# Induced attention and an ELU feed-forward on one core: which engine takes off the 1 of 1+elu, and where it is made up for

## The chip, the cores and the metric

One core of one Trainium2 chip. The engines run side by side and meet through semaphores: TensorE (PE, matmuls into PSUM, the memory of the matmul sums), VectorE (DVE), ScalarE (ACT), GpSimd (POOL, which works on SBUF, the main on-chip memory) and SyncE (SP, which here issues the DMA transfers). The metric is device microseconds of one execution; lower is better.

## The reference

```python
B, N, m, C = 4, 12480, 32, 128                     # x: (B, N, C), inducing: (m, C)
def mab(q, kv):
    s = scale * (q @ kv.transpose(0, 2, 1))
    s = s - s.max(-1, keepdims=True)
    a = np.exp(s)
    a /= a.sum(-1, keepdims=True) + 1e-09
    return a @ kv
h = mab(I, x)                                      # 32 rows look at all of x
x = mab(x, h).reshape(B * N, C)                    # every token looks at those 32 rows
h = x @ w_in                                       # (49920, 128) @ (128, 2048)
g = np.where(h > 0.0, h, np.exp(np.minimum(h, 0.0)) - 1.0)
return (g @ w_out).astype(np.float32)              # (49920, 2048) @ (2048, 128)
```

x and inducing are float32; the two weights are float64 and are put into float32 on the chip. Nearly all of the work is the last three lines.

## The kernel before

**Tiles.** The tokens of a batch are cut into 25 blocks, 15 of 512 and 10 of 480 (GROUPING), so there are 60 and 40 blocks in the four batches. The 2048 hidden columns are 16 chunks of 128, taken in pairs. A *unit* is one block and one pair (8 units a block, 800 in all), and nearly all instructions work on a unit's tile of 128 x 1024 (or 960).

**A unit.** `ffn_in` (L618) makes ph = h + 1 with two matmuls in PSUM (the 1 comes from rows of ones in `hw` and in the stacks; w_in is folded into the 32 attended rows, so the contraction has 128 rows). ACT then makes e = exp(ph - 1) (L626). `ffn_mid` (L632, DVE) makes min(max(ph, 1), e), which is 1 + elu(h). The rest depends on the pair's letter in PLAN:

- N: POOL subtracts 1 in place (L653), and e goes as it is, float32, into two full matmuls with `wo_n`. The profile shows a float32 matmul as two instructions.
- P and D are *split*: ACT writes gh, elu rounded to F32R, a shorter float32 that PE takes in one instruction (`ffn_split`, L641, bias -1), then somebody writes the remainder gl, and the product is summed from gh x wo_h, gh x wo_l and gl x wo_h: six matmuls a unit. For D, DVE makes gl = (g - 1) - gh (L648); here `ffn_mid` has written g over ph, so L648 reads PSUM and SBUF, and the PSUM tile stays taken until then. For P, POOL first subtracts 1 in place (L653), then makes gl = e - gh (L658).

PLAN is PDNPDPND: three P, three D, two N. Chunks of P and D have their places in `wo_h` and `wo_l` (CHUNKS_S), those of N in `wo_n`. All 16 chunks of a block are summed in one PSUM bank, `po` (L680), one of two that take turns. After the eighth pair DVE transposes `po` into `o` in SBUF (L688), and SP writes it out with four DMAs (L692).

**Order.** PE, DVE and ACT run in the order in which the program is written; POOL and SP are put in order by the framework, and tiles are handed out from pools: three PSUM tiles for ph, five for e, four for gh, four for gl, two for o. One step of the unit loop issues `ffn_in(n)` with its exponential, `ffn_mid(n - 1)`, `ffn_split(n - 1)`, `ffn_low(n - 2)`, what is due of the attention steps, and `ffn_out(n - 5)`. So ACT's queue is exponential n, split n - 1; DVE's is L632 of n - 1, L648 of n - 2.

**Attention.** The two attentions of the next batch and the next groups of blocks are side steps with written due times in units of blocks (`attend`, `first_half`). The second attention comes per group of two to four blocks and uses POOL three times: subtracting the maximum (L550), dividing (L570), and the remainder of the rounded weights (L591); stacks of weights are then copied by DMA (L596).

**Start.** The first 105 us or so make the float32 weights out of the float64 bits (class `Weight`, `split_w_out`) and the first attention of batch 0, in the order of the text FIRST; DVE and POOL have instructions there with two operands in SBUF (L198, L208, L212, L239).

Of the kernel before, what the change touches and what calls it, by code (L numbers as in the profile page):

```python
# [9 lines left out]
F32 = mybir.dt.float32  # L10
F32R = mybir.dt.float32r
I32 = mybir.dt.int32
U32 = mybir.dt.uint32
AF = mybir.ActivationFunctionType
# [4 lines left out]
Q = 32  # L19
# [5 lines left out]

PLAN = "PDNPDPND"

# [13 lines left out]
def kernel(  # L45
# [28 lines left out]
    NFC = F // P  # L74
    NCP = NFC // 2
    assert len(PLAN) == NCP
    CHUNKS_S = [f for f in range(NFC) if PLAN[f // 2] != "N"]
    CHUNKS_N = [f for f in range(NFC) if PLAN[f // 2] == "N"]
    WHERE_S = {f: i for i, f in enumerate(CHUNKS_S)}
    WHERE_N = {f: i for i, f in enumerate(CHUNKS_N)}  # L80
# [34 lines left out]
    def bank(name, take=False):  # L115
        if not steady and not take:
            return ps_h.tile([P, 2, 512], F32, tag="ph", name=name)[:, 0]
        t = ps_o.tile([P, 512], F32, tag=f"po{turn[0] % 2}", name=name)
        if take:
            turn[0] += 1  # L120
        return t
# [29 lines left out]
    wo_n = const.tile([P, len(CHUNKS_N), C], F32, name="wo_n")  # L151
    wo_h = const.tile([P, NSPLIT, C], F32R, name="wo_h")
    wo_l = const.tile([P, NSPLIT, C], F32R, name="wo_l")
    WS = 512
    rebias = const.tile([P, 1], F32, name="rebias")
    nc.gpsimd.memset(rebias, -896.0)
# [451 lines left out]
    def plan(n):  # L608
        b, k, cp = units[n]
        return PLAN[cp]  # L610
# [17 lines left out]

    def ffn_mid(n):
        v = live[n]  # L630
        v["g"] = v["ph"] if plan(n) == "D" else v["e"]
        nc.vector.scalar_tensor_tensor(  # L632
            out=v["g"], in0=v["ph"], scalar=1.0, in1=v["e"], op0=ALU.max, op1=ALU.min
        )

    def ffn_split(n):
        v, how = live[n], plan(n)
        shape = list(v["e"].shape)
        if how != "N":
            v["gh"] = ghp.tile(shape, F32R, tag="gh", name=f"gh_{n}")  # L640
            nc.scalar.activation(v["gh"], v["g"], AF.Copy, bias=-1.0)  # L641

    def ffn_low(n):
        v, how = live[n], plan(n)
        shape = list(v["e"].shape)
        if how == "D":
            v["gl"] = glp.tile(shape, F32R, tag="gl", name=f"gl_{n}")
            nc.vector.scalar_tensor_tensor(  # L648
                out=v["gl"], in0=v["g"], scalar=-1.0, in1=v["gh"].bitcast(F32),
                op0=ALU.add, op1=ALU.subtract,  # L650
            )
        else:
            nc.gpsimd.tensor_scalar(  # L653
                out=v["e"], in0=v["e"], scalar1=-1.0, scalar2=1.0, op0=ALU.add, op1=ALU.mult
            )
        if how == "P":
            v["gl"] = glp.tile(shape, F32R, tag="gl", name=f"gl_{n}")
            nc.gpsimd.tensor_sub(v["gl"], v["e"], v["gh"].bitcast(F32))  # L658

    def ffn_out(n):  # L660
        b, k, cp = units[n]
# [7 lines left out]
        for i in range(2):  # L669
# [3 lines left out]
            else:  # L673
# [2 lines left out]
                parts.append((1, wo_l[:, w, :], v["gh"][:, i]))  # L676
                parts.append((2, wo_h[:, w, :], v["gl"][:, i]))
        parts.sort(key=lambda v: v[0])
        for i, (_, w, g) in enumerate(parts):
            nc.tensor.matmul(  # L680
                po[:, :T], w, g,
                start=(cp == 0 and i == 0),
                stop=(cp == NCP - 1 and i == len(parts) - 1),
            )
        if cp == NCP - 1:
            yield 1
            o = op.tile([P, U, Q], F32, tag="o", name=f"o_{b}_{k}")
            nc.vector.transpose(o.rearrange("p u d -> p (u d)"), po[:, :T])  # L688
            at = b * N + BLOCKS[k][0]
            dst = out[at : at + T, :]  # L690
            for dq in range(4):
                nc.sync.dma_start(  # L692
                    dst[:, dq * Q : (dq + 1) * Q].rearrange("(u t) d -> t u d", t=Q),
                    o[dq * Q : (dq + 1) * Q, :, :],
                )
# [194 lines left out]
```

## Time and profile before

| | us |
|---|---|
| median of 3 runs | 1710.24 |
| lowest, highest | 1710.19, 1712.89 |
| span of the profiled execution | 1710.8 |

| engine | busy us | share of the span | instructions |
|---|---|---|---|
| PE (matmuls) | 1656.3 | 97% | 7448 |
| PEld (weight loads, beside the matmuls) | 1176.5 | 69% | 7448 |
| DVE | 1522.5 | 89% | 1575 |
| ACT | 1390.6 | 81% | 1620 |
| POOL | 1342.3 | 78% | 948 |

Times in rows are microseconds unless marked ns. A row of the groups reads: line, engine, operation, tile written <- tiles read, shapes, count | busy time, mean ns of one | idle time of the engine before them, and what ended it. A row of the timeline reads: start, duration, engine, line, operation, tiles, shapes, count. A row of waits reads: who <- whom: microseconds in all, times, longest. The stretch view gives each engine's busy time in a stretch with its count of instructions. A matmul's end is modelled, so what one costs is read from start to start.

### The profile page before, as it was taken

What the parts mean: (1) busy time and instruction counts of PE and PEld (TensorE: products, weight loads), DVE (VectorE), ACT (ScalarE), POOL (GpSimd) and SP (SyncE); (2) the same over time, 40 slices, a digit from 0 to 9 for tenths busy, and PEclk for the clock granted to TensorE, in tenths of its full rate; (3) what the DMA queues carried; (4) which work ended last, traced back from release to release, by engine and by line L of the source; (5) the groups of instructions that cost most, each with busy time, mean ns of one, the idle gap of its engine ahead of it and who ended that gap; (6) DMA issues with size and microseconds to landing.
All of it is one profiled execution on the core that took longest, in us unless ns stands there. A gap on an engine that the chain in (4) does not pass through costs nothing.

```text
span 1710.8 us, 22335 instructions
## 1 busy us (share of the span) xinstructions
PE 1656.3 (97%) x7448; PEld 1176.5 (69%) x7448; DVE 1522.5 (89%) x1575; ACT 1390.6 (81%) x1620; POOL 1342.3 (78%) x948
## 2 busy tenths in 40 slices
PE   6589999999999999999999999999999999999998
PEld 4356776677776776767776676677777677777776
DVE  5799899898899998988989999889888989998996
ACT  4378888888787888888888888888878888888886
POOL 4488787787797877877888787787778888888886
PEclk9699999999999999999999999999999999999999
DMA  7144223322324233232223332321222111111111
GB/s 249 35 91 80 56 43 78 63 48 70 70 46 83 37 75 70 45 62 58 71 64 54 65 62 53 75 55 21 74 49 40 35 20 36 28 37 19 36 25 19
DMA packets 384754, 98.10 MB, mean 57 GB/s; under 512 B 364864, under 2 KB 370784, under 8 KB 384384
## 3 DMA queue, kind: packets, MB, share of 16 engines
q1 hardware_dynamic: 384640, 96.68, 27.9%
q8 instruction: 59, 0.97, 0.2%
q14 instruction: 55, 0.45, 0.1%
HBM read 48.94 MB, written 25.56 MB: 44 GB/s over the span
## 4 chain that ended last, share of the span: by engine, by line
PE 87%; DVE 7%; ACT 3%; issue 2%; DMA 1%; POOL 0%; SPq 0%; DVEq 0%; ACTq 0%
PE po L680 62%; PE ph L618 20%; ACT e L626 2%; DVE e L632 1%; PE ps_s L312 1%; PE ps_t L531 1%; PE ps_hh L403 1%; DVE ph L632 1%; ACT gh L641 1%; DMA xm<-in_x_dram 1%; DVE o L688 1%; DVE w_part L198 1%; DVE gl L648 0%; DMA w_raw<-in_moe_w_in_dram 0%; PE ps_hw L467 0%
## 5 line engine op out<-in xcount | busy, mean ns | idle before, releaser
L626 ACT ACTIVATE e<-ph 128x1024 f32<-128x1024 f32 (+1 forms) x800 | 803.4, 1005 | 228.8 <-PE ph L618 223.7
L653 POOL TENSOR_SCALAR e<-e 128x1024 f32<-128x1024 f32 (+1 forms) x500 | 510.8, 1029 | 280.6 <-ACT gh L641 270.4
L658 POOL TENSOR_TENSOR gl<-e,gh 128x1024 fp32r<-128x1024 f32 (+1 forms) x300 | 703.8, 2346 | 16.8
L632 DVE SCALAR_TENSOR_TENSOR e<-ph,e 128x1024 f32<-128x1024 f32 (+1 forms) x500 | 594.5, 1189 | 88.0 <-ACT e L626 84.9
L618 PE MATMUL ph<-stk,hw 128*128 128x512 f32 (+1 forms) x1600 | 566.8, 436 | 15.8 <-DVE e L632 9.6
L680 PE MATMUL po<-gh,wo_h 128*128 128x512 f32 (+1 forms) x1200 | 469.2, 391 | 7.5 <-ACT wo_h L238 3.5
L680 PE MATMUL po<-gh,wo_l 128*128 128x512 f32 (+1 forms) x1200 | 469.3, 391 | 6.6 <-POOL wo_l L239 6.6
L618 PEld LDWEIGHTS ph<-stk,hw 128*128 128x128 f32 x1600 | 295.4, 189 | 188.9 <-issue 84.9
L632 DVE SCALAR_TENSOR_TENSOR ph<-ph,e 128x1024 f32<-128x1024 f32 (+1 forms) x300 | 359.3, 1198 | 63.1 <-ACT e L626 62.3
L680 PE MATMUL po<-gl,wo_h 128*128 128x512 f32 (+1 forms) x1200 | 371.1, 390 | 0.7 <-POOL gl L658 0.7
L680 PE MATMUL po<-e,wo_n 128*128 128x512 f32 (+1 forms) x800 | 367.8, 582 | 0.1
L648 DVE SCALAR_TENSOR_TENSOR gl<-ph,gh 128x1024 fp32r<-128x1024 f32 (+1 forms) x300 | 356.3, 1188 | 1.0 <-ACT gh L641 1.0
L641 ACT ACTIVATE gh<-e 128x1024 fp32r<-128x1024 f32 (+1 forms) x300 | 311.3, 1038 | 13.9 <-DVE e L632 13.5
L641 ACT ACTIVATE gh<-ph 128x1024 fp32r<-128x1024 f32 (+1 forms) x300 | 300.6, 1002 | 19.1 <-DVE ph L632 18.2
L680 PEld LDWEIGHTS po<-gh,wo_h 128*128 128x128 f32 x1200 | 225.9, 188 | 56.6 <-issue 7.4
L680 PEld LDWEIGHTS po<-gh,wo_l 128*128 128x128 f32 x1200 | 225.9, 188 | 56.5 <-POOL wo_l L239 8.2
L680 PEld LDWEIGHTS po<-gl,wo_h 128*128 128x128 f32 x1200 | 225.6, 188 | 49.1 <-POOL gl L658 1.7
L680 PEld LDWEIGHTS po<-e,wo_n 128*128 128x128 f32 x800 | 150.6, 189 | 106.3 <-issue 91.3
L688 DVE STREAM_TRANSPOSE o<-po 128x512 f32<-128x512 f32 (+1 forms) x100 | 69.1, 691 | 4.0 <-PE po L680 4.0
L259 DVE STREAM_TRANSPOSE xT<-xq 128x1024 f32<-128x1024 f32 (+2 forms) x39 | 45.5, 1166 | 0.0
L570 POOL TENSOR_TENSOR s<-s,sm 128x512 f32<-128x512 f32 (+3 forms) x27 | 27.7, 1027 | 19.3 <-DVE sm L569 19.3
L403 PEld LDWEIGHTS ps_hh<-xm,e 128*32 128x32 f32 (+2 forms) x872 | 24.6, 115 | 16.9 <-issue 12.3
(99 smaller groups left out, 557.5 us busy)
## 6 DMA issues: line engine op xcount, KB each, us to landing
xm<-in_x_dram SPq DMA_DIRECT2D x32, 512.0 KB, 4.8
out_dram<-o SPq DMA_DIRECT2D x240, 64.0 KB, 2.0
xq<-in_x_dram SPq DMA_DIRECT2D x84, 128.0 KB, 2.9
out_dram<-o SPq DMA_DIRECT2D x160, 60.0 KB, 2.0
stk<-ahi SPq DMA_DIRECT2D x118, 64.0 KB, 2.0
xq<-in_x_dram SPq DMA_DIRECT2D x60, 120.0 KB, 2.8
stk<-ahi SPq DMA_DIRECT2D x80, 60.0 KB, 2.0
stk<-alo SPq DMA_DIRECT2D x59, 64.0 KB, 2.0
```

What stands on the lines that cost most here:

```text
L259: nc.vector.transpose(t, xq.rearrange("p u d -> p (u d)"))
L403: nc.tensor.matmul(ps[c * Q : (c + 1) * Q, :C], st["e", g][:np_, u * Q : (u + 1) * Q], st["xm", g, u - u % UP][:np_, u % UP, :], start=(u ...
L570: eng.tensor_tensor(out=s, in0=s, in1=sm.unsqueeze(2).broadcast_to([np_, U, Q]), op=ALU.mult)
L618: nc.tensor.matmul(ph[:, i], state[b]["hw"][:, f * P : (f + 1) * P], stacks[b, k], start=True, stop=True,)
L626: nc.scalar.activation(e, ph, AF.Exp, bias=-1.0)
L632: nc.vector.scalar_tensor_tensor(out=v["g"], in0=v["ph"], scalar=1.0, in1=v["e"], op0=ALU.max, op1=ALU.min)
L641: nc.scalar.activation(v["gh"], v["g"], AF.Copy, bias=-1.0)
L648: nc.vector.scalar_tensor_tensor(out=v["gl"], in0=v["g"], scalar=-1.0, in1=v["gh"].bitcast(F32), op0=ALU.add, op1=ALU.subtract,)
L653: nc.gpsimd.tensor_scalar(out=v["e"], in0=v["e"], scalar1=-1.0, scalar2=1.0, op0=ALU.add, op1=ALU.mult)
L658: nc.gpsimd.tensor_sub(v["gl"], v["e"], v["gh"].bitcast(F32))
L680: nc.tensor.matmul(po[:, :T], w, g, start=(cp == 0 and i == 0), stop=(cp == NCP - 1 and i == len(parts) - 1),)
L688: nc.vector.transpose(o.rearrange("p u d -> p (u d)"), po[:, :T])
```

## The change

- PLAN becomes PPNPDPDP: five P, two D, one N.
- P no longer subtracts 1: gh is 1 + elu rounded, and gl the remainder of 1 + elu. N doesn't subtract either, so its matmuls take 1 + elu. L653 is gone. D still subtracts 1, on ACT for gh and on DVE for gl.
- Each output element has thus become too large by the sum of the `w_out` rows of the P and N chunks. `sum_excess` makes these sums once, ahead of the output matmuls of the first block's last pair: a tile of ones (POOL) times the parts of the weights on PE, in rounded matmuls for `wo_h` and `wo_l` and a full one for `wo_n`, and four reduces on DVE. CHUNKS_S lists P's chunks first, so that they lie side by side.
- Each output tile `o` has the sums taken off by POOL, between DVE's transpose and the DMAs.
- `ffn_mid` writes e for all pairs, so D's middle result lies in SBUF and the PSUM tile is free after it; D's remainder on DVE then reads two SBUF tiles.

```diff
-PLAN = "PDNPDPND"
+PLAN = "PPNPDPDP"
...
-    CHUNKS_S = [f for f in range(NFC) if PLAN[f // 2] != "N"]
+    CHUNKS_S = [f for how in "PD" for f in range(NFC) if PLAN[f // 2] == how]
...
     def ffn_mid(n):
         v = live[n]
-        v["g"] = v["ph"] if plan(n) == "D" else v["e"]
         nc.vector.scalar_tensor_tensor(
-            out=v["g"], in0=v["ph"], scalar=1.0, in1=v["e"], op0=ALU.max, op1=ALU.min
+            out=v["e"], in0=v.pop("ph"), scalar=1.0, in1=v["e"], op0=ALU.max, op1=ALU.min
         )
...
-            nc.scalar.activation(v["gh"], v["g"], AF.Copy, bias=-1.0)
+            nc.scalar.activation(v["gh"], v["e"], AF.Copy, bias=0.0 if how == "P" else -1.0)
...
         if how == "D":
             v["gl"] = glp.tile(shape, F32R, tag="gl", name=f"gl_{n}")
             nc.vector.scalar_tensor_tensor(
-                out=v["gl"], in0=v["g"], scalar=-1.0, in1=v["gh"].bitcast(F32),
+                out=v["gl"], in0=v["e"], scalar=-1.0, in1=v["gh"].bitcast(F32),
                 op0=ALU.add, op1=ALU.subtract,
-            )
-        else:
-            nc.gpsimd.tensor_scalar(
-                out=v["e"], in0=v["e"], scalar1=-1.0, scalar2=1.0, op0=ALU.add, op1=ALU.mult
             )
...
+    def sum_excess():
+        ones = ep.tile([P, TM], F32, tag="e", name="ones")[:, :P]
+        ones_r = ones.bitcast(F32R)
+        nc.gpsimd.memset(ones, 1.0)
+        n_p = sum(PLAN[f // 2] == "P" for f in CHUNKS_S)
+        n_n = len(CHUNKS_N)
+        parts = [
+            (ones_r, w[:, i : min(i + 4, n_p), :]) for w in (wo_h, wo_l) for i in range(0, n_p, 4)
+        ]
+        parts += [(ones, wo_n[:, i : min(i + 4, n_n), :]) for i in range(0, n_n, 4)]
+        ps = bank("ps_excess")
+        for i, (one, w) in enumerate(parts):
+            m = w.shape[1] * C
+            nc.tensor.matmul(
+                ps[:, :m], one, w.rearrange("p c d -> p (c d)"),
+                start=i == 0, stop=i == len(parts) - 1,
+            )
+        for dq in range(4):
+            rows = slice(dq * Q, (dq + 1) * Q)
+            nc.vector.tensor_reduce(
+                out=excess[rows],
+                in_=ps.rearrange("p (c d) -> p d c", d=C)[rows, rows, :],
+                axis=AX.X, op=ALU.add,
+            )
...
+        if n == NCP - 1:
+            sum_excess()
...
             o = op.tile([P, U, Q], F32, tag="o", name=f"o_{b}_{k}")
             nc.vector.transpose(o.rearrange("p u d -> p (u d)"), po[:, :T])
+            nc.gpsimd.tensor_tensor(
+                out=o, in0=o, in1=excess.unsqueeze(1).broadcast_to([P, U, Q]), op=ALU.subtract
+            )
```

More of the change, by code (lines that the diff above doesn't have):

```diff
@@ L153 @@
     wo_l = const.tile([P, NSPLIT, C], F32R, name="wo_l")
+    excess = const.tile([P, Q], F32, name="excess")
     WS = 512
```

## The prediction

> **What bounds the kernel now.** I read the stretch view first, for 1600 us in the middle that leave out the start and the tail, then what TensorE (PE) waits for in the same stretch.
>
> ```profile
> span 1710.8 us, 22335 instructions
> ```
> ```profile
> core 0: us, PE busy (x) PEld busy (x) DVE busy (x) ACT busy (x) POOL busy (x), PEclk, DMA share, GB/s
> 105.00:1705.00 1600.00, 1591.84 (x6988) 1136.65 (x6987) 1445.00 (x1452) 1342.68 (x1536) 1285.49 (x884) 1.00 0.27 52
> ```
> ```profile
> PE ph L618 <- DVE e L632: 4.2, 8, 0.9
> ...
> PE po L680 <- POOL wo_l L239: 6.6, 2, 4.1
> ```
>
> PE is busy 99.5% of the stretch at full clock, and its longest sum of waits from 105 us on is 4.2 us (first row; the second belongs to the start, and prices a wait there below). So PE's work sets the time; VectorE (DVE) is at 90%, ScalarE (ACT) at 84%, GpSimd (POOL) at 80%. Every microsecond taken from PE counts until one of these has none left.
>
> What a pair costs PE is read from start to start in PE's timeline, since the ends are modelled. First blocks of 480 tokens, then 512:
>
> ```profile
> 901.89 1.77 PE L680 MATMUL po<-e,wo_n 128*128 128x480 f32 x4
> 903.12 0.99 PE L618 MATMUL ph<-stk,hw 128*128 128x512 f32 x2
> 903.96 0.38 PE L680 MATMUL po<-gh,wo_h 128*128 128x480 f32 x1
> ...
> 905.72 0.38 PE L680 MATMUL po<-gh,wo_h 128*128 128x480 f32 x1
> ...
> 907.49 0.38 PE L680 MATMUL po<-gh,wo_h 128*128 128x480 f32 x1
> ...
> 915.13 0.39 PE L680 MATMUL po<-gh,wo_h 128*128 128x512 f32 x1
> ...
> 916.52 0.62 PE L618 MATMUL ph<-stk,hw 128*128 128x512 f32 x2
> 916.98 1.88 PE L680 MATMUL po<-e,wo_n 128*128 128x512 f32 x4
> 918.29 1.03 PE L618 MATMUL ph<-stk,hw 128*128 128x512 f32 x2
> 919.16 0.39 PE L680 MATMUL po<-gh,wo_h 128*128 128x512 f32 x1
> ```
>
> Output matmuls plus the next pair's two input matmuls: at 512, split 916.98 - 915.13 = 1.85 us, unsplit 919.16 - 916.98 = 2.18 us; at 480, split 907.49 - 905.72 = 1.77, unsplit 903.96 - 901.89 = 2.07. Six rounded matmuls are cheaper than two full ones.
>
> **The change, part by part.** *PE.* One of eight pairs goes from unsplit to split: 0.33 us in each of the 60 blocks of 512 and 0.30 in each of the 40 of 480, together -31.8 us. Once, in the first block, the sum of the weights is added: rounded matmuls over 2 x (512 + 512 + 256) columns, five times 0.23 us (a sixth of 916.52 - 915.13), 1.15 us, and one full matmul over 256 columns, a quarter of the unsplit pair's 2.18 - 0.46 (the input pair, 916.98 - 916.52), 0.43: +1.6. Before it PE waits for a memset of POOL at a time when POOL is busy, behind which stand all later matmuls. No such wait is in the trace; the lower bound is nothing, the upper 4.1 us, the longest wait of PE for POOL in the start. I take +1.5, nearer to nothing, since that one needed four instructions. The four reduces on DVE behind it touch only the other output bank, so I count nothing (under 1 us if not hidden).
>
> *ACT.* Seven instead of six splits per block, all from SBUF.
>
> ```profile
> 906.89 1.07 ACT L641 ACTIVATE gh<-e 128x1024 fp32r<-128x1024 f32 x1
> 907.84 1.04 ACT L626 ACTIVATE e<-ph 128x1024 f32<-128x1024 f32 x1
> 908.74 1.05 ACT L641 ACTIVATE gh<-ph 128x1024 fp32r<-128x1024 f32 x1
> ```
>
> A split takes 0.95 us of the engine, an exponential 0.90. 99 blocks lie in the stretch (297 of L648, row below, three a block), so ACT rises by about 94 to 1437 us. That is hidden under PE's new 1600 - 31.5 = 1568 us, at 92%; a pair costs ACT 1.85 us and PE 1.85, so a run of split pairs gives ACT no slack and only the unsplit pair and the attention steps do.
>
> *POOL.* The subtraction of 1 goes (five a block), the low halves rise from three to five a block, and one subtraction over the output tile is added.
>
> ```profile
> L653 POOL TENSOR_SCALAR e<-e 128x1024 f32<-128x1024 f32 (+1 forms) x500 | 510.8, 1029 | 280.6 <-ACT gh L641 270.4
> L658 POOL TENSOR_TENSOR gl<-e,gh 128x1024 fp32r<-128x1024 f32 (+1 forms) x300 | 703.8, 2346 | 16.8
> ...
> L648 DVE SCALAR_TENSOR_TENSOR gl<-ph,gh 128x1024 fp32r<-128x1024 f32 (+1 forms) x300 | 356.3, 1188 | 1.0 <-ACT gh L641 1.0
> ```
> ```profile
> L591 POOL TENSOR_TENSOR alo<-aT,ahi 128x512 fp32r<-128x512 f32 x11 | 14.3, 1297 | 0.7 <-ACT ahi L589 0.7
> ...
> L570 POOL TENSOR_TENSOR s<-s,sm 128x512 f32<-128x512 f32 x11 | 11.6, 1052 | 9.0 <-DVE sm L569 9.0
> ```
>
> The added one lies between the 1.05 us of L570 (one operand broadcast, f32 out, as here) and the 1.30 of L591; I take 1.05. Per block -5 x 1.029 + 2 x 2.346 + 1.05 = +0.60 us, 59 in the stretch: 1285.5 + 59 = 1345 us, 86% of 1568 (1369, 87%, at 1.30). The output DMAs now wait for it; behind them on SyncE stand the loads of x and the copies into the stacks, which are issued blocks ahead. It costs only at the end, where the last tile's DMAs come +1.05 later.
>
> *DVE.* L648 alone, in the same stretch:
>
> ```profile
> 105.00:1705.00 1600.00, 352.69 (x297) 1.00 0.27 52
> ```
>
> One of the three low halves a block goes, a third of 352.7, -118: 1327 us, 85%. Its middle result in SBUF instead of PSUM leaves the duration alone (L632's two forms have the same shape) and frees the PSUM tile after L632 instead of after L648, which removes waits that were 4.2 us at most.
>
> **The part that speaks against it.** The low half on DVE (L648) reads one operand from PSUM and one from SBUF now; after the change both from SBUF. DVE, then POOL, in the start of the run, where DVE has instructions with two SBUF operands (L198, L208, L570):
>
> ```profile
> 69.75 0.68 DVE L198 SCALAR_TENSOR_TENSOR w_part<-w_raw,w_part 128x512 uint32<-128x512 uint32 x1
> ...
> 70.94 0.69 DVE L208 SCALAR_TENSOR_TENSOR w_raw<-w_raw 128x512 f32<-128x512 uint32 x1
> ...
> 72.87 1.46 DVE L570 TENSOR_TENSOR s<-s,sm 96x512 f32<-96x512 f32 x1
> ...
> 96.81 2.69 DVE L198 SCALAR_TENSOR_TENSOR w_part<-w_raw,w_part 128x512 uint32<-128x512 uint32 x1
> ```
> ```profile
> 71.03 1.50 POOL L653 TENSOR_SCALAR e<-e 128x1024 f32<-128x1024 f32 x1 [6.43 <-ACT gh L641]
> 72.50 1.28 POOL L212 TENSOR_TENSOR w_raw<-w_raw,w_part 128x512 f32<-128x512 f32 x1
> 73.75 2.79 POOL L658 TENSOR_TENSOR gl<-e,gh 128x1024 fp32r<-128x1024 f32 x1
> ...
> 96.61 2.34 POOL L658 TENSOR_TENSOR gl<-e,gh 128x1024 fp32r<-128x1024 f32 x1
> 98.91 2.80 POOL L239 TENSOR_TENSOR wo_l<-w_raw,wo_h 128x128 fp32r<-128x128 f32 x4
> ```
>
> L198 takes 0.68 us alone; at 96.81, begun 0.2 us into POOL's L658, it takes 2.69 and ends at 99.50, 0.55 after POOL is done. L653 started 0.09 us behind L208 takes 1.50 instead of 1.03; L658 started beside the waiting L570 takes 2.79 instead of the 2.42 of the one at 914.93 below. So the two exclude each other for a whole instruction, and whoever waits goes next. Today's low halves are free of it:
>
> ```profile
> 914.66 1.22 DVE L632 SCALAR_TENSOR_TENSOR e<-ph,e 128x1024 f32<-128x1024 f32 x1
> 915.80 1.21 DVE L648 SCALAR_TENSOR_TENSOR gl<-ph,gh 128x1024 fp32r<-128x1024 f32 x1
> 916.93 1.21 DVE L632 SCALAR_TENSOR_TENSOR e<-ph,e 128x1024 f32<-128x1024 f32 x1
> ```
> ```profile
> 914.93 2.42 POOL L658 TENSOR_TENSOR gl<-e,gh 128x1024 fp32r<-128x1024 f32 x1
> ```
>
> L648 at 915.80 runs in 1.21 us through the middle of a POOL instruction. After the change it would wait until 917.35, 1.55 us, and behind it stand L632 of the next pair, its split on ACT, and so POOL's next low half.
>
> The Trainium skill, "SBUF — State Buffer", section "SBUF: two separate sides", says the same: a DVE instruction with two SBUF inputs and a GpSimd instruction that reads SBUF share a port pair as an exclusive lock, held for the whole instruction. The rows agree; read literally, the rule makes each of the 198 DVE low halves a full 1.19 us loss for POOL, and the time the 1728 us of the third case below.
>
> How much POOL loses to one low half is bounded by the rows: L658 lost 0.37 us to L570's 512 elements; 512 more at the 0.53 us by which L648 exceeds L198 (1.21 - 0.68) make 0.90; the whole instruction is 1.19. I take the middle, 1.05, since 0.37 comes from one pair: 198 x 1.05 = 208 us. POOL must also wait for its inputs. With pairs 1.86 us apart, a low half on POOL is ready some 4.05 us after its exponential begins (the next pair's exponential ends at 2.8, the split at 3.8, and hand-overs), so the run of pairs 7, 0, 1 keeps POOL busy from 4.05 to 11.1 after pair 7's start, and pair 3's is ready at 4 x 1.86 + 4.05 = 11.5: 0.4 us idle a block when POOL is on time, nothing when it is late. I take 0.3, 30 us in the stretch. Sum: 1345 + 208 + 30 = 1583 us, where PE needs 1568: POOL with this exclusion ends last, by 15 us.
>
> **The sum.** 1710.8 - 31.8 + 1.6 + 1.5 + 1.05 = 1683 us with PE as the bound; + 15 for the exclusion = 1698 us. The profiled execution (1710.8) stands 0.6 us over the median of the runs (1710.24), so no correction is made. A change of less than 0.2% (1706.8 to 1713.7) could not be told from none.
>
> **The rivals.**
> *1. PE stays the bound: 1683 us.* It needs POOL's loss below (1568 - 1345) / 198 = 1.13 us a low half with no idle, or 0.98 with my 30 us. For it: 0.90 is the only bound that starts from a measured loss; pairs 4 and 6, the DVE ones, each follow a POOL pair whose low half is ending when DVE comes (at 4.5 against 4.0 us after the pair's start), so waits are half a microsecond; a PSUM tile is free once L632 is done, 2.2 us after its exponential began, and is wanted by PE three pairs on, at 3 x 1.86 - 0.46 = 5.1, so DVE may be 2.9 us late before PE waits. Against: 86% of POOL's time leaves little to catch up after the three attention steps (1.05 + 1.05 + 1.30 us) that fall in every fourth block.
> *2. My forecast, part of the gain kept: 1698 us.*
> *3. The exclusion costs more than the matmuls give: slower.* If each low half takes the whole 1.19 us from POOL, 1345 + 236 + 30 = 1611, 43 over PE's 1568: 1726 to 1728 us. It decides from 1683 + (1375 + 198 h - 1568) = 1713.7, h = 1.13 us. DVE's side says the same: 1327 + 198 x 1.2 of waiting = 1565, no slack left; at the 1.55 read above, 1634 and 1749 us.
> *4. ACT becomes the bound.* Four tiles for high halves serve runs of seven split pairs now; the split of pair n then needs the output matmuls of pair n - 4, which end at 1.86 + 1.40 = 3.26 us against ACT's 2.77. Three such pairs a block lose 0.5 us each if nothing is caught up: 1437 + 149 = 1586, 18 over: 1701 us. The loss should be paid once, as both run at 1.85 afterwards.
>
> **How the numbers follow.** PE bound 0.27, my forecast 0.38, exclusion worse 0.27, ACT 0.08. My forecast's own range is 1683 to 1712 (h from 0.98 to 1.12). Faster by over 0.2%: all of the first, 0.31 of the second, 0.04 of the last, 0.62; same: 0.07 of the second, 0.03 of the third, 0.02 of the last, 0.12; slower 0.26. The range reaches from 1679 (the first case without the start's waits) to 1738, between the two prices of the third.
>
> **What would show it.** PE: L680 with wo_n x400, the others x1400, and the distance between pairs 1.85 us. POOL: no L653; its low halves 2.35 us, some longer by 0.4 to 1.2. DVE: L648's mean above 1.19, at about 1.7; at 1.19 the exclusion is absent and 1683 follows, above 2.4 the third case. PE's waits: near nothing in the first case; on POOL's gl or DVE's e in the second and third; on ACT's gh in the fourth. I am wrong altogether if the distance between split pairs grows without any wait, or if the low halves wait and PE doesn't.

## The result, and the profile after

The changed kernel takes 1757.3 us (median of 4 runs, 1757.09 to 1760.81) against 1710.2: a ratio of 1.0276 [1.0261, 1.0290]. It is 2.8% slower, 59 us over the forecast and 19 us above the range. Lines of the kernel have moved: the exponential is now L627, the split L641, the input matmuls L619, the output matmuls L703, the transpose L711, the new subtraction L712; the low half on DVE is still L648, that on POOL is L654.

The page of the changed kernel (span; the engines' busy time; the chain that ended last, by engine; the costliest groups, as busy us, mean ns of one, idle time ahead and what ended it):

```profile
span 1755.4 us, 23030 instructions
...
PE 1650.4 (94%) x7656; PEld 1216.8 (69%) x7656; DVE 1552.8 (88%) x1479; ACT 1490.1 (85%) x1720; POOL 1521.8 (87%) x751
...
PE 46%; DVE 28%; ACT 11%; issue 9%; POOL 2%; DMA 2%; SPq 0%; ACTq 0%; POOLq 0%; DVEq 0%
...
L654 POOL TENSOR_TENSOR gl<-e,gh 128x1024 fp32r<-128x1024 f32 (+1 forms) x500 | 1194.4, 2401 | 177.1 <-ACT gh L641 163.5
...
L641 ACT ACTIVATE gh<-e 128x1024 fp32r<-128x1024 f32 (+1 forms) x700 | 724.4, 1035 | 152.3 <-DVE e L632 140.0
L627 ACT ACTIVATE e<-ph 128x1024 f32<-128x1024 f32 (+1 forms) x800 | 792.0, 996 | 53.0 <-PE ph L619 50.8
...
L648 DVE SCALAR_TENSOR_TENSOR gl<-e,gh 128x1024 fp32r<-128x1024 f32 (+1 forms) x200 | 379.7, 1899 | 0.2
...
L712 POOL TENSOR_TENSOR o<-o,excess 128x512 f32<-128x512 f32 (+1 forms) x100 | 197.8, 1978 | 3.1 <-DVE o L711 3.1
```

The chain of before went over PE for 87% of its length and over DVE for 7%. Now it is 46%, 28% and 11% on ACT: no engine sets the end alone, and the chain changes engine at hand-overs. L648's mean rose from 1.19 to 1.90 us, and its idle time is 0.2 us for 200 of them: **the wait for the other engine is recorded inside the instruction**, so it shows in no list of waits. The same holds for L712, 1.98 us in the mean where its shortest take 1.2 to 1.3.

The stretch view, on the columns that the prediction showed for before:

```profile
105.00:1750.00 1645.00, 1586.84 (x7194) 1176.30 (x7194) 1474.89 (x1358) 1441.55 (x1635) 1464.70 (x690) 0.99 0.26 51
```

PE is busy 96.5% of it, after 99.5%. DVE's 90% holds its waits. What others wait for, in the lists of waits of the changed kernel and of the kernel before (us in all, times, longest):

```profile
ACT gh L641 <- DVE e L632: 140.0, 196, 4.8
ACT e L627 <- PE ph L619: 50.8, 58, 5.1
PE ph L619 <- DVE e L632: 37.0, 32, 4.8
```
```profile
ACT e L626 <- PE ph L618: 223.7, 235, 2.6
...
ACT gh L641 <- DVE ph L632: 18.2, 32, 3.2
...
ACT gh L641 <- DVE e L632: 13.5, 21, 3.3
```

Before, ACT's idle time was nearly all for PE: ACT was ahead, and PE the bound. Now ACT's splits wait 140.0 us for DVE's middle step where they waited 18.2 + 13.5 = 31.7, and its waits for PE are down to 50.8.

How one late low half travels is best seen at the longest one. DVE, POOL, ACT and PE in the timeline of the changed kernel (start, length; in brackets the idle time before and who ended it):

```profile
1495.74 1.23 DVE L632 SCALAR_TENSOR_TENSOR e<-ph,e 128x1024 f32<-128x1024 f32 x1 [0.18 <-ACT e L627]
1496.88 6.19 DVE L648 SCALAR_TENSOR_TENSOR gl<-e,gh 128x1024 fp32r<-128x1024 f32 x1
1503.00 2.34 DVE L632 SCALAR_TENSOR_TENSOR e<-ph,e 128x1024 f32<-128x1024 f32 x2
```
```profile
1496.03 2.38 POOL L654 TENSOR_TENSOR gl<-e,gh 128x1024 fp32r<-128x1024 f32 x1
1498.38 1.29 POOL L712 TENSOR_TENSOR o<-o,excess 128x512 f32<-128x512 f32 x1
1499.64 2.35 POOL L654 TENSOR_TENSOR gl<-e,gh 128x1024 fp32r<-128x1024 f32 x1
```
```profile
1498.44 1.03 ACT L627 ACTIVATE e<-ph 128x1024 f32<-128x1024 f32 x1
1504.24 1.06 ACT L641 ACTIVATE gh<-e 128x1024 fp32r<-128x1024 f32 x1 [4.77 <-DVE e L632]
```
```profile
1504.26 1.21 PE L619 MATMUL ph<-stk,hw 128*128 128x512 f32 x2 [3.87 <-DVE e L632]
```

L648 comes at 1496.88, 0.85 us into POOL's L654, and runs 6.19 us: through the rest of that one, through L712 and through the next L654, which ends at 1501.99. Two POOL instructions went ahead of a DVE instruction that was already there. Behind L648 stand the middle steps of the next two pairs; behind the first of these stands ACT's split, 4.77 us; behind that split, in ACT's own queue, the next exponential; and PE waits 3.87 us for a PSUM tile, which is free only after the middle step. Behind this wait the granted clock of PE is at half for a while (stretch view; the clock stands third from the end, after POOL's busy time):

```profile
1504.40:1507.60 3.20, 3.20 (x8) 2.55 (x9) 3.20 (x3) 3.20 (x4) 0.36 (x1) 0.50 0.00 0
```

The ordinary case is milder. DVE and POOL 50 us later:

```profile
1550.17 2.04 DVE L648 SCALAR_TENSOR_TENSOR gl<-e,gh 128x1024 fp32r<-128x1024 f32 x1
```
```profile
1548.73 2.41 POOL L654 TENSOR_TENSOR gl<-e,gh 128x1024 fp32r<-128x1024 f32 x1
1551.07 2.31 POOL L712 TENSOR_TENSOR o<-o,excess 128x512 f32<-128x512 f32 x1
```

DVE waits until L654 is done, goes next, and POOL's subtraction waits for DVE. Counted over the trace, 40 of the 200 low halves take under 1.3 us, 55 take 1.3 to 1.8, 85 take 1.8 to 2.5, 15 take 2.5 to 3.8, and 5 take 5.46 to 6.19.

### The profile page after: what moved, and what is told of

It is laid out like the page before. It is cut to its first block, busy times and chain, and to the rows that moved or that the text cites. A ratio compares the mean times of both kernels' runs of the same rounds, so it can differ in the third digit from the quotient of the medians.

```text
span 1755.4 us, 23030 instructions
## 1 busy us (share of the span) xinstructions
PE 1650.4 (94%) x7656; PEld 1216.8 (69%) x7656; DVE 1552.8 (88%) x1479; ACT 1490.1 (85%) x1720; POOL 1521.8 (87%) x751
## 4 chain that ended last, share of the span: by engine, by line
PE 46%; DVE 28%; ACT 11%; issue 9%; POOL 2%; DMA 2%; SPq 0%; ACTq 0%; POOLq 0%; DVEq 0%
PE po L703 32%; DVE e L632 14%; PE ph L619 11%; DVE gl L648 9%; ACT e L627 6%; ACT gh L641 4%; POOL gl L654 1%; DVE xT L260 1%; DVE o L711 1%; DMA xm<-in_x_dram 1%; PE ps_s L313 1%; POOL o L712 1%; PE ps_t L532 1%; PE ps_hh L404 1%; DVE s L542 0%
## 5 line engine op out<-in xcount | busy, mean ns | idle before, releaser
L654 POOL TENSOR_TENSOR gl<-e,gh 128x1024 fp32r<-128x1024 f32 (+1 forms) x500 | 1194.4, 2401 | 177.1 <-ACT gh L641 163.5
L632 DVE SCALAR_TENSOR_TENSOR e<-ph,e 128x1024 f32<-128x1024 f32 (+1 forms) x800 | 938.4, 1185 | 154.7 <-ACT e L627 152.6
L641 ACT ACTIVATE gh<-e 128x1024 fp32r<-128x1024 f32 (+1 forms) x700 | 724.4, 1035 | 152.3 <-DVE e L632 140.0
L627 ACT ACTIVATE e<-ph 128x1024 f32<-128x1024 f32 (+1 forms) x800 | 792.0, 996 | 53.0 <-PE ph L619 50.8
L619 PE MATMUL ph<-stk,hw 128*128 128x512 f32 (+1 forms) x1600 | 547.7, 424 | 43.4 <-DVE e L632 37.0
L703 PE MATMUL po<-gh,wo_h 128*128 128x512 f32 (+1 forms) x1400 | 551.2, 394 | 14.7 <-ACT wo_h L239 7.3
L703 PE MATMUL po<-gh,wo_l 128*128 128x512 f32 (+1 forms) x1400 | 550.4, 393 | 3.9 <-POOL wo_l L240 3.9
L703 PE MATMUL po<-gl,wo_h 128*128 128x512 f32 (+1 forms) x1400 | 435.6, 392 | 3.2 <-POOL gl L654 3.2
L619 PEld LDWEIGHTS ph<-stk,hw 128*128 128x128 f32 x1600 | 292.4, 190 | 204.1 <-issue 75.4
L648 DVE SCALAR_TENSOR_TENSOR gl<-e,gh 128x1024 fp32r<-128x1024 f32 (+1 forms) x200 | 379.7, 1899 | 0.2
L703 PEld LDWEIGHTS po<-gh,wo_h 128*128 128x128 f32 x1400 | 265.3, 189 | 76.8 <-issue 11.9
L703 PEld LDWEIGHTS po<-gl,wo_h 128*128 128x128 f32 x1400 | 264.9, 190 | 63.2 <-POOL gl L654 5.9
L703 PEld LDWEIGHTS po<-gh,wo_l 128*128 128x128 f32 x1400 | 265.2, 189 | 58.4 <-POOL wo_l L240 5.4
L712 POOL TENSOR_TENSOR o<-o,excess 128x512 f32<-128x512 f32 (+1 forms) x100 | 197.8, 1978 | 3.1 <-DVE o L711 3.1
L703 PE MATMUL po<-e,wo_n 128*128 128x512 f32 (+1 forms) x400 | 184.6, 584 | 0.0
L703 PEld LDWEIGHTS po<-e,wo_n 128*128 128x128 f32 x400 | 75.6, 190 | 53.9 <-issue 46.4
L711 DVE STREAM_TRANSPOSE o<-po 128x512 f32<-128x512 f32 (+1 forms) x100 | 68.8, 688 | 2.9 <-PE po L703 2.9
L592 POOL TENSOR_TENSOR alo<-aT,ahi 128x512 fp32r<-128x512 f32 (+3 forms) x27 | 36.9, 1366 | 0.0
```

The source lines that it names most:

```text
L592: eng.tensor_sub(alo, aT, ahi.bitcast(F32))
L619: nc.tensor.matmul(ph[:, i], state[b]["hw"][:, f * P : (f + 1) * P], stacks[b, k], start=True, stop=True,)
L627: nc.scalar.activation(e, ph, AF.Exp, bias=-1.0)
L632: nc.vector.scalar_tensor_tensor(out=v["e"], in0=v.pop("ph"), scalar=1.0, in1=v["e"], op0=ALU.max, op1=ALU.min)
L641: nc.scalar.activation(v["gh"], v["e"], AF.Copy, bias=0.0 if how == "P" else -1.0)
L648: nc.vector.scalar_tensor_tensor(out=v["gl"], in0=v["e"], scalar=-1.0, in1=v["gh"].bitcast(F32), op0=ALU.add, op1=ALU.subtract,)
```

## The experiments

The theory after the result: DVE's low half, with both operands in SBUF, and POOL's instructions exclude each other; the delay, not POOL's lost time, makes the kernel slower, through the split on ACT. Rivals: it is the sums or the new order of pairs; it is POOL's amount of work; the exclusion matters only where POOL's instructions follow each other without a gap; ACT is nothing but a place through which the delay passes, with time to spare. The texts quoted name theories by letters; each result is told in words.

Times are medians; the kernel before stood beside all of them at 1710.1 to 1710.7.

| kernel | us | ratio to before [95%] |
|---|---|---|
| changed kernel | 1757.3 | 1.0276 [1.0261, 1.0290] |
| D's middle result in PSUM | 1694.4 | 0.9905 [0.9888, 0.9921] |
| kernel before, D's middle result in SBUF | 1837.4 | 1.0740 [1.0724, 1.0756] |
| changed, no subtraction | 1693.6 | 0.9898 [0.9883, 0.9913] |
| changed, half a subtraction | 1707.0 | 0.9976 [0.9966, 0.9987] |
| changed, subtraction later in POOL's queue | 1799.1 | 1.0518 [1.0503, 1.0534] |
| PSUM, old plan | 1715.1 | 1.0027 [1.0017, 1.0037] |
| PSUM, the sums' reduces a pair later | 1693.3 | 0.9898 [0.9881, 0.9915] |
| PSUM, no subtraction | 1692.5 | 0.9894 [0.9879, 0.9909] |
| PSUM, two subtractions | 1696.1 | 0.9911 [0.9896, 0.9926] |
| PSUM, DVE busier ahead of its low halves | 1731.3 | 1.0116 [1.0101, 1.0131] |
| PSUM, ACT busier at both D pairs | 1752.2 | 1.0246 [1.0229, 1.0263] |
| PSUM, ACT busier at one D pair | 1718.4 | 1.0049 [1.0034, 1.0064] |

### One operand back in PSUM

The changed kernel with the middle result of D's pairs written over `ph` again:

```diff
+        v["g"] = v["ph"] if plan(n) == "D" else v["e"]
-            out=v["e"], in0=v.pop("ph"), scalar=1.0, in1=v["e"], op0=ALU.max, op1=ALU.min
+            out=v["g"], in0=v.pop("ph"), scalar=1.0, in1=v["e"], op0=ALU.max, op1=ALU.min
...
-            nc.scalar.activation(v["gh"], v["e"], AF.Copy, bias=0.0 if how == "P" else -1.0)
+            nc.scalar.activation(v["gh"], v["g"], AF.Copy, bias=0.0 if how == "P" else -1.0)
...
-                out=v["gl"], in0=v["e"], scalar=-1.0, in1=v["gh"].bitcast(F32),
+                out=v["gl"], in0=v["g"], scalar=-1.0, in1=v["gh"].bitcast(F32),
```

> The changed kernel with one thing undone: the middle result of the two DVE pairs stays in PSUM, so L648's counterpart reads PSUM and SBUF. Theory A (the exclusion of DVE's two-SBUF low half and GpSimd, whose waits run through DVE's queue into ScalarE's): the low half takes 1.19 us again instead of 1.90, TensorE is the bound, 1683 us by the prediction's own sum, 1680 to 1692. Theory B (ScalarE has no slack left: seven splits a block, runs of seven split pairs on four tiles for high halves): nothing changes for ScalarE, 1740 to 1757 us.

1694.4 us: faster than before by 0.95%, and 62.9 us faster than the changed kernel. Its groups, then its stretch and its waits:

```profile
L649 DVE SCALAR_TENSOR_TENSOR gl<-ph,gh 128x1024 fp32r<-128x1024 f32 (+1 forms) x200 | 237.4, 1187 | 0.1
...
L655 POOL TENSOR_TENSOR gl<-e,gh 128x1024 fp32r<-128x1024 f32 (+1 forms) x500 | 1168.6, 2354 | 214.0 <-ACT gh L642 199.6
...
L713 POOL TENSOR_TENSOR o<-o,excess 128x512 f32<-128x512 f32 (+1 forms) x100 | 126.3, 1263 | 3.9 <-DVE o L712 3.9
```
```profile
105.00:1680.00 1575.00, 1560.66 (x7172) 1171.77 (x7173) 1349.21 (x1357) 1428.87 (x1635) 1361.82 (x688) 1.00 0.27 53
```
```profile
ACT e L627 <- PE ph L619: 121.4, 160, 5.1
...
ACT gh L642 <- DVE e L633: 25.4, 49, 3.8
...
ACT gh L642 <- DVE ph L633: 3.9, 12, 0.5
```

The low half is back at 1.19 us, the subtraction at 1.26, ACT's waits for DVE at 29.3 us, and PE is busy 99.1% of its stretch. So the whole loss hangs on where that one operand lies. All other parts of the change are in this kernel, and with them it gains. One more thing moves with the operand: ACT's splits of D's pairs take 1.005 us from PSUM and 1.035 from SBUF, 6 us over the run. That isn't the loss, for the changed kernel without the subtraction, below, has them in SBUF too and loses nothing.

### The middle result in SBUF, alone

The kernel before, with only this part of the change:

```diff
-        v["g"] = v["ph"] if plan(n) == "D" else v["e"]
+        v["g"] = v["e"]
-            out=v["g"], in0=v["ph"], scalar=1.0, in1=v["e"], op0=ALU.max, op1=ALU.min
+            out=v["g"], in0=v.pop("ph"), scalar=1.0, in1=v["e"], op0=ALU.max, op1=ALU.min
```

> The kernel before with one part of the change alone: the middle result of its three DVE pairs lies in SBUF. Theory A: its 300 low halves wait for GpSimd as the 200 of the changed kernel do, 1.8 to 2.2 us each instead of 1.19; DVE's 1445 us of the middle stretch become 1630 to 1740 where 1600 were the bound: 1735 to 1790 us. Theory B: six splits a block as before and PSUM free sooner, 1710 us.

1837.4 us, above what was expected. The page:

```profile
PE 1697.7 (92%) x7448; PEld 1170.1 (64%) x7448; DVE 1759.1 (96%) x1575; ACT 1413.6 (77%) x1620; POOL 1512.2 (82%) x948
...
L648 DVE SCALAR_TENSOR_TENSOR gl<-e,gh 128x1024 fp32r<-128x1024 f32 (+1 forms) x300 | 610.2, 2034 | 1.5 <-ACT gh L641 1.1
L653 POOL TENSOR_SCALAR e<-e 128x1024 f32<-128x1024 f32 (+1 forms) x500 | 651.0, 1303 | 236.4 <-ACT gh L641 197.9
```

Three low halves a block wait here, 0.85 us each, and POOL's own subtraction of 1 went from 1.03 to 1.30 us. DVE, its waits counted as busy, is full at 96%. The part that costs the changed kernel 63 us costs 127 in the old order of pairs.

### Without the new subtraction

The changed kernel without the three lines at L712:

```diff
-            nc.gpsimd.tensor_tensor(
-                out=o, in0=o, in1=excess.unsqueeze(1).broadcast_to([P, U, Q]), op=ALU.subtract
-            )
```

> The changed kernel without GpSimd's subtraction over the output tile; the output then keeps the sum of the weights that should come off. Theory A: the low halves of DVE still wait behind GpSimd's low halves, but the second of the two a block meets a free GpSimd more often; part of the loss goes, 1715 to 1745 us. If it was GpSimd's amount of work that set the time (89% busy in the middle stretch, 1.98 us a block for this operation), 1690 us or less. Theory B: 1750 us or more.

1693.6 us. I had expected a part of the loss to go; all of it went, with the middle result still in SBUF. The groups and the waits:

```profile
L648 DVE SCALAR_TENSOR_TENSOR gl<-e,gh 128x1024 fp32r<-128x1024 f32 (+1 forms) x200 | 298.0, 1490 | 0.2
```
```profile
ACT gh L641 <- DVE e L632: 70.4, 141, 4.2
...
ACT e L627 <- PE ph L619: 68.0, 78, 5.1
```

Low halves still wait, 0.30 us in the mean, and ACT waits 41 us more for DVE than with PSUM, at no cost in time. So a wait of 0.30 us was hidden and one of 0.71 was not. The same subtraction left out of the PSUM kernel completes the square:

> The middle result of DVE's pairs in PSUM, and GpSimd's subtraction over the output tile left out (the output keeps the sum of the weights). With e1_psum, the changed kernel and e3_no_subtract this makes a square of two things. Theory A1 and A2: with PSUM there is no exclusion, so the subtraction lies under TensorE's work and only its 1.05 to 1.3 us at the end go, with the hand-over 2.4 at most: 1690 to 1694 us. If the subtraction itself held the kernel up (GpSimd at 86%), 1680 or less.

1692.5. The subtraction costs 1.9 us with PSUM (1694.4 - 1692.5) and 63.7 with SBUF (1757.3 - 1693.6): all but 1.9 of it comes only together with the exclusion.

### Is it POOL's amount of work?

The PSUM kernel with a second subtraction, of a tile of zeros, behind the first:

```diff
+            nc.gpsimd.tensor_tensor(
+                out=o, in0=o, in1=nothing.unsqueeze(1).broadcast_to([P, U, Q]), op=ALU.subtract
+            )
```

> The kernel of e1_psum with a second instruction of the same kind on GpSimd behind the subtraction (it takes off a tile of zeros): GpSimd has 1362 + 125 us of work in 1575, 94%, more than in the changed kernel (1465 in 1645, 89%), and no exclusion. Theory C and D: with PSUM nothing couples the two, 1694 to 1702 us. Theory A2 (GpSimd's amount of work sets the time): 1740 us or more.

1696.1, with POOL busy 94% of its stretch:

```profile
105.00:1690.00 1585.00, 1566.58 (x7194) 1174.66 (x7194) 1349.98 (x1358) 1429.97 (x1635) 1487.58 (x790) 1.00 0.27 53
```

POOL is not the bound, even with more work than it has in the changed kernel (89% of the stretch, its waits counted as busy). The other way, the PSUM kernel with the old plan:

```diff
-PLAN = "PPNPDPDP"
+PLAN = "PDNPDPND"
```

> The changed kernel with the old plan PDNPDPND and the middle result in PSUM: what is left of the change is GpSimd's subtraction of 1 taken away (500 x 1.03 us), the sums in the start and the subtraction over the output tile (100 x 1.05 us). TensorE is the bound in the middle, so GpSimd's 4 us a block less give nothing there, and the start and the end cost the prediction's 1.6 + 1.5 + 1.05 us: 1714 us, 1710 to 1717. Theory A and B say the same; under 1705 would mean that GpSimd held TensorE up before.

1715.1, as expected in all; POOL is busy 56% of the span and nothing is gained by that. The total is in part luck: a batch in the middle takes 1.0 us more than before (410.59 against 409.60, from one batch's first exponential to the next one's), which was not forecast, and the start less than forecast. No run shows what takes the 1.0.

### Half a subtraction, and a later one

The changed kernel, with the subtraction over half of the columns:

```diff
+            h = U // 2
-                out=o, in0=o, in1=excess.unsqueeze(1).broadcast_to([P, U, Q]), op=ALU.subtract
+                out=o[:, :h], in0=o[:, :h], in1=excess.unsqueeze(1).broadcast_to([P, h, Q]),
+                op=ALU.subtract,
```

> The changed kernel with the subtraction over half of the output tile only (the other half keeps the sum of the weights): about 0.65 us of GpSimd instead of 1.26, in the same place. Between 1693.6 us (none) and 1757 us (all) this says whether the loss grows with GpSimd's time: half of it, 1715 to 1735 us, under theory D; a step, within 5 us of one of the two ends, if only the order of the queues matters.

1707.0, below the expected 1715 to 1735, with 1.62 us for a low half:

```profile
L648 DVE SCALAR_TENSOR_TENSOR gl<-e,gh 128x1024 fp32r<-128x1024 f32 (+1 forms) x200 | 323.2, 1616 | 0.2
```
```profile
ACT gh L641 <- DVE e L632: 88.1, 193, 4.1
```

So there is no jump between no subtraction and a whole one: the cost grows with the wait, from a point on. Then the whole subtraction six steps later in the block's schedule and behind POOL's latest low half in POOL's queue, so that it would stand away from DVE's low halves:

```diff
+            if n < len(units) - 1:
+                yield 6
+            with tc.issue_after(latest[0].ins):
-            nc.gpsimd.tensor_tensor(
-                out=o, in0=o, in1=excess.unsqueeze(1).broadcast_to([P, U, Q]), op=ALU.subtract
-            )
+                nc.gpsimd.tensor_tensor(
+                    out=o, in0=o, in1=excess.unsqueeze(1).broadcast_to([P, U, Q]), op=ALU.subtract
+                )
```

> The changed kernel (middle results in SBUF) with GpSimd's subtraction over the output tile six pairs later, so that on GpSimd's queue it stands between the low halves of pairs 1 and 3 of the next block but one, instead of between those of pairs 3 and 5, where DVE's two low halves come. The same instructions on every engine. Theory A1 (what costs is that this one stands where DVE's low halves want the port, which makes GpSimd's next low half late and DVE's second one wait for all of it): nearly all of the loss goes, 1693 to 1712 us, and the mean of L648 falls to about 1.5 us as without the subtraction. Theory A2 (GpSimd's amount of work with the exclusion on top is what does not fit): 1740 to 1760 us.

1799.1, which neither expectation allowed. POOL's timeline, then the group of DVE's low halves and the waits:

```profile
1448.68 13.98 POOL L656 TENSOR_TENSOR gl<-e,gh 128x1024 fp32r<-128x1024 f32 x5
```
```profile
L650 DVE SCALAR_TENSOR_TENSOR gl<-e,gh 128x1024 fp32r<-128x1024 f32 (+1 forms) x200 | 411.8, 2059 | 0.1
```
```profile
ACT gh L641 <- DVE e L632: 123.6, 162, 4.2
ACT e L627 <- DVE gl L650: 62.9, 34, 4.6
```

Moved away from the place where they meet, the subtraction made POOL late: in this stretch five of its low halves run without a gap, and DVE's fall into such runs. Of the two low halves of a block on DVE, the second gained by the move (1.47 us in the mean, 1.84 in the changed kernel) and the first lost more (2.64, 1.96 in the changed kernel). The mean of 2.06 us is the largest of the two-low-half kernels, and a new wait appears, the exponential for DVE's low half. Only the place of one POOL instruction, with the output DMAs behind it, differs, and it is worth 42 us. Why this place brings just this much isn't settled.

### Does DVE's delay alone do it?

The PSUM kernel, where nothing excludes anything, with a reduce over half of `gh` that nobody reads ahead of DVE's low half:

```diff
+            unread = small.tile([P, 1], F32, tag="unread", name=f"unread_{n}")
+            nc.vector.tensor_reduce(
+                out=unread, in_=v["gh"][:, 0].bitcast(F32), axis=AX.X, op=ALU.max
+            )
```

> The kernel of e1_psum (no exclusion) with an added instruction on DVE ahead of each of its low halves: a maximum over 512 columns of the rounded half, whose result nobody reads, about 0.67 us, which is the 0.71 us by which the changed kernel's low halves are longer; it has one SBUF operand, so GpSimd isn't held. Theory C (the time is lost in DVE's queue: 0.7 us twice a block make the next pairs' L632, then ScalarE's splits late, and ScalarE, with seven splits a block, can't make that up): 1735 to 1760 us, as the changed kernel. Theory D (it takes GpSimd's loss and lateness as well, the two holding each other): 1694 to 1710 us.

The added reduce in the groups, and the waits:

```profile
L649 DVE TENSOR_REDUCE unread<-gh 128x1 f32<-128x512 f32 (+1 forms) x200 | 132.9, 665 | 0.0
```
```profile
ACT gh L642 <- DVE e L633: 78.2, 147, 4.5
...
ACT gh L642 <- DVE ph L633: 33.9, 81, 1.1
...
ACT e L627 <- PE ph L619: 64.4, 77, 5.1
```

1731.3: between the two expected ranges. The reduce takes 0.67 us, but the low half starts 0.58 us after it, so the steady delay is 0.58 us where the changed kernel's mean is 0.71. It makes 36.9 of the 62.9 us (1731.3 - 1694.4), with the same signs on ACT. So DVE's lateness alone, with POOL left in peace, is more than half of it.

The other 26 us go with the exclusion: in part with the delay that is larger by 0.13, in part with its unevenness. The changed kernel's trace shows where: from 105 us on PE idles 58.7 us, here 39.5, with PSUM 16.1. Eight waits of PE of 1.8 to 3.9 us, 22.6 us together, each come behind a low half of DVE that POOL had passed; from 120 us on PE's longest here is 1.4. Behind the four longest, of 3.6 us and more, PE's granted clock is at half for 3.4 us each, as in the row at 1504.40; here and in the PSUM kernel it is full from 114 us to the tail. An estimate from these rows is 6.8 us at most for that (half of 4 x 3.4). No run separates the unevenness, the slower clock and POOL's own lost time.

### Has ACT time to spare?

The PSUM kernel, with the first half of D's tile rounded twice on ACT, at both D pairs, and then at pair 4 alone:

```diff
+            if how == "D":
+                nc.scalar.activation(v["gh"][:, 0], v["g"][:, 0], AF.Copy, bias=-1.0)
```
```diff
+            if how == "D" and units[n][2] == 4:
+                nc.scalar.activation(v["gh"][:, 0], v["g"][:, 0], AF.Copy, bias=-1.0)
```

> The kernel of e1_psum (no exclusion) with an added instruction on ScalarE ahead of the split of each of the two DVE pairs of a block: the first half of the tile is rounded twice, about 0.52 us from start to start, 104 us in all. Over the runs so far the time above e1_psum goes with ScalarE's waits for DVE: 41 us more waiting costs nothing, 59 cost 13, 83 cost 37, 111 cost 63, 157 cost 105, that is all but 41 to 53 us. Theory E (ScalarE has about 47 us to give, whatever takes them): 1694 + 104 - 47 = 1751 us, 1741 to 1758. Theory F (the waits go with the loss but it is made in DVE's and GpSimd's queues; ScalarE waits 121 us for TensorE in e1_psum, so 104 fit): 1694 to 1702 us.

> As e11_psum_busy_act, at one of the two DVE pairs only: 52 us more of ScalarE. Theory E: at the edge of what it has to give, 1694 + 5 = 1699 us, 1694 to 1705. Theory F: 1694 to 1697 us. A time near 1720 (half of the loss of e11_psum_busy_act) would say that there is no threshold.

The engines' busy time on the page of the first, then of the second:

```profile
PE 1652.8 (94%) x7656; PEld 1208.1 (69%) x7656; DVE 1441.9 (82%) x1479; ACT 1582.1 (90%) x1920; POOL 1418.8 (81%) x751
```
```profile
PE 1644.0 (96%) x7656; PEld 1212.5 (71%) x7656; DVE 1434.8 (84%) x1479; ACT 1531.8 (89%) x1820; POOL 1420.5 (83%) x751
```

ACT is busy 104 us more than in the PSUM kernel (1582.1 against 1478.0), 1.04 a block, and the kernel takes 57.8 us more, 1752.2: nearly what the changed kernel loses, with DVE and POOL free of each other. With one pair it is 54 us more (1531.8) and 23.9 us of time, 1718.4, where both theories had said at most 1705. So ACT has no store of some 47 us that is used up first: of the first 54 us 44% show, of the next 50 us 67% (33.9 us more). Less than 54 was not tried. ACT's waits do not count in the same way: without the subtraction it waits 41 us more for DVE, at no cost.

### The sums' reduces a pair later

In the PSUM kernel the four reduces of the sums stand in DVE's queue ahead of work of the next pair. Moved one pair on, by a step of the generator ahead of them and a call in front of the first block's transpose:

```diff
+        yield 1
         for dq in range(4):
...
-            sum_excess()
+            sums = sum_excess()
+            next(sums)
...
+            if n == NCP - 1:
+                list(sums)
```

> The kernel of e1_psum with the four reduces of the sums one pair later in DVE's queue. In e1_psum DVE stands idle for 5.8 us in the start, with the next pairs' work behind it, until TensorE, itself late for the last weights, has made the sums. If that wait is what the start costs over the prediction's 3.1 us, TensorE finds its tiles sooner: 1688 to 1692 us. If TensorE only waits for the output bank instead, or was held by the weights, 1693 to 1696 us.

1693.3 against 1694.4, whose runs lie between 1692.8 and 1695.7: no difference that can be told. The reduces cost nothing to speak of.

## Why the prediction was wrong

**PE's gain: right, and near its size.** 31.8 us on the whole are 7.95 for each of the four batches. The same exponential of a block of the second batch and of the third, 25 blocks later, in ACT's timelines of the kernel before (of two in one row, both times), the PSUM kernel and the changed kernel:

```profile
526.17 2.19 ACT L626 ACTIVATE e<-ph 128x1024 f32<-128x1024 f32 x2
...
935.77 2.19 ACT L626 ACTIVATE e<-ph 128x1024 f32<-128x1024 f32 x2
```
```profile
527.61 1.05 ACT L627 ACTIVATE e<-ph 128x1024 f32<-128x1024 f32 x1
...
930.65 1.05 ACT L627 ACTIVATE e<-ph 128x1024 f32<-128x1024 f32 x1
```
```profile
539.00 1.03 ACT L627 ACTIVATE e<-ph 128x1024 f32<-128x1024 f32 x1
...
955.85 1.03 ACT L627 ACTIVATE e<-ph 128x1024 f32<-128x1024 f32 x1
```

409.60, 403.04 and 416.85 us a batch. With PSUM 6.6 us are gained. With the old plan and the rest of the change a batch took 410.59, so the pair that goes from unsplit to split is worth 7.55, and the rest of the change takes 1.0 a batch, which the sum did not have. The changed kernel has the same matmuls as the PSUM kernel and pays 13.8 on top. The last batch pays most: from the first exponential of its third block to that of its last it takes 331.7 us with PSUM and 357.5 after.

**Start and end: a term missing in the start.** 3.1 us were forecast for the start (matmuls and memset). The third block's first exponential comes at 118.04 us before, at 119.14 with the sums in the old plan, and at 124.39 in the PSUM kernel: the sums cost 1.1, and the new plan, for which the sum had nothing in the start, 5.2 more. With it PE's granted clock is at half until 113 us, with the old plan and the sums until 104.5; which of the two, the clock or the lateness, brought the other isn't shown. The reduces at nothing were right. So was the end: the last block takes 1.2 us longer in the old plan with the sums, forecast 1.05. With 6.6 for 7.95 (5.4 us in all) and 3.2 more in the start, the -27.65 of the first rival become -19; between the spans of the two profiled executions, 1710.8 and 1691.6, lie 19.2. The medians are only 16.3 apart: the prediction held the span of 1710.8 to be 0.6 us over the median, but a span leaves out some 1.8 us of an execution (1755.4 of 1757.21), so before's profile was one of its longer runs.

**The part against it: the cause was right.** Two SBUF operands on DVE and POOL's instructions exclude each other: L648 1.90 against 1.19 us, and both times that the operand alone was moved decide it. The forecast of 1.7 for L648's mean was near. The Trainium skill, "SBUF — State Buffer", section "SBUF: two separate sides", has it as an exclusive lock held for a whole instruction, with the other side blocked. The trace agrees as to the blocking (L712 at 1551.07 takes 2.31 us behind L648, against 1.26 without exclusion).

**The step that failed: where the exclusion is paid.** The prediction put the price on POOL's capacity, "1.05" us lost per DVE low half, 208 us. Measured on POOL: its low halves grew from 2.354 to 2.401 us (500 times, 24 us) and the subtraction from 1.263 to 1.978 (100 times, 72 us), 95 us in all or 0.48 a low half. POOL still had 177 us idle ahead of its low halves, and 94% of the stretch did not bind it in the run with two subtractions. POOL lost half of what was forecast, and a busier POOL does not set the time: 127 us more of work on it cost 1.7 us (1696.1 - 1694.4). So the term of the sum that failed is the +15 for the exclusion: it measures 62.9 (1757.3 - 1694.4).

The price is DVE's delay and what waits behind it on ACT and PE. Delaying DVE alone, with POOL left in peace, already turns the gain into a loss (1731.3). Three sentences of the prediction passed over it:
- *"waits are half a microsecond"*, and DVE "may be 2.9 us late before PE waits". The mean wait is 0.71, with five above 4. And PE isn't the only one that waits: so does the split, which stands in ACT's queue ahead of the next exponential.
- *ACT "is hidden under PE's new" time at 92%*. The prediction itself had 1.85 us per pair for both ACT and PE, and then counted ACT as hidden since its total is lower. The runs with a busier ACT show that about half of what is added to ACT comes through. How much of the loss takes this way is not shown: PE also waits for DVE's middle step itself, for the PSUM tile (28.8 us from 105 us on, 4.3 with PSUM), and no run separates the two.
- *"whoever waits goes next"*. In 20 cases POOL's next instruction passed a waiting low half (15 times the subtraction behind a low half of POOL); at the boundary of POOL's low half to L712 DVE went next in 73 others.

How the time follows ACT's waits for DVE (the sum of the rows shown; the exponential's wait for L650 included), each against the PSUM kernel's 29.3 us and 1694.4:

| kernel | ACT's waits for DVE, more | time, more |
|---|---|---|
| no subtraction | 41 | -1 |
| half | 59 | 13 |
| DVE busier | 83 | 37 |
| changed | 111 | 63 |
| subtraction later | 157 | 105 |

The time grows by 42 to 52 us less than these waits; ACT's waits for PE, 121.4 us in the PSUM kernel, are 50.8 to 68.0 in the others. In part this must be so, since ACT's busy time, nearly the same in these (1478 to 1492 us), and its waits add up to the span; it says where the time lies. That DVE's delay is the cause is shown by the run that delays DVE alone, for 37 of the 63 us.

**The rivals.** The third named the exclusion with a worse price; its side was right, its sizes (1726 to 1728 on POOL, 1749 from DVE's capacity) short of 1757, for it too went by an engine's total. The fourth had ACT near its limit, by another way, the four tiles: the changed kernel's splits wait 8.6 us for the output matmuls, so that was small.

**Open.** What decides that POOL passes a waiting DVE instruction: neither how long POOL's next instruction had been ready nor the time at which DVE came sorts the 20 from the others. In all 15 at that boundary POOL's low half had itself begun without idle time ahead of it, but so it had in 48 of the 73. How the last 26 us divide between the uneven waits, PE's slower clock behind the longest and POOL's lost time. And whether the delay reaches PE by way of ACT or straight from DVE.

The best kernel of these that leaves nothing out is the changed one with one operand left in PSUM, 1694.4 us, 0.95% under the kernel before; with the reduces a pair later it is as fast.

## What to carry to other kernels

Where GpSimd is busy, leave one operand of VectorE's two-input instructions in PSUM: here that is worth 63 us of 1757, or 127 in the other order of pairs. When an engine's total is 92% of the bound's, compare also what one step costs each: with 1.85 us a pair on both, ACT passed on 44% of the first 54 us of work that were added to it, and more of the next 50. Follow a delay along the queues, instruction by instruction, to what stands behind the one that waits, before any engine's total is used as a price.

## What was not expected of the hardware

A waiting VectorE instruction can be passed by two GpSimd instructions in a row: 6.19 us for one that takes 1.19. It isn't first come, first served: at the boundary of a low half to the subtraction the subtraction went ahead of a waiting VectorE 15 times, and VectorE went next 73 times; behind five of those 15 a second GpSimd instruction passed too.

The wait counts as busy time of the waiting engine. DVE's stretch rose from 1349 to 1475 us with the same work (1357 and 1358 instructions), 142 us of it over the whole run in L648 alone, with 0.2 us of idle time ahead of it; neither the list of waits nor the idle column of that group shows it. Only the mean of the group, beside the same group of another kernel, does.
